# Residual loads two steps earlier and attention visits re-spaced in a strided-attention plus feed-forward kernel

## The chip, the cores and the metric

The kernel runs on one core of a Trainium2 chip. The metric is the device time of one execution in microseconds (us), lower is better. Times of several runs are given as a median with their lowest and highest; the profile is one further execution taken by the hardware profiler.

## What is computed

Attention over 8 batches, 8 heads, 576 positions, 64 wide: the first four heads see a causal band of 32 positions, the last four see causal positions at a stride of 32. Its output, as 4608 rows of 512, goes through a layer norm, a feed-forward of 512 to 2048 to 512 with ReLU, and a residual.

```
scores = np.where(masks, scale * q @ k.T, -1e9)
attn   = softmax(scores)
x      = (attn @ v) as rows of 512
out    = x + relu(layernorm(x) * g_ln @ w_ch1) @ w_ch2
```

## The kernel before

The feed-forward goes over 9 chunks of 512 rows (a chunk is the first 512 rows of a batch, the ninth gathers the eight remainders). A chunk has 16 steps, f = 0 to 15. One step of chunk c is: `ffn1` (L800 to L821), 12 matmuls of 128x512 into the one buffer `ph`; `h_high` on ACT (`hh`, L825) and `h_low` on DVE (`hl`, L830), which empty `ph`; one piece of attention work taken from a generator (`next(gen, None)`); then `second(*prev)`, that is `ffn2` (L840) of the step before, 12 matmuls into the four outputs `po`. At f = 15 of a chunk `ffn2` is followed by `finish` (L846, DVE), which adds the residual `x` and stores it; because of the lag by one step this lies in f = 0 of the next chunk. Every float32 product is made of three passes with high and low parts, hence the 12.

Chunk 0 follows an order written by hand (the string `ORDER`). Chunks 1 to 6 run the loop just described, and I number their steps 0 to 95 (step = 16 times (c - 1) + f). Chunks 7 and 8 run at the end in a different form, with seven products of half matrices (L1137) that need sums of weights and of x prepared during chunks 2 to 6.

The attention is spread over steps 0 to 95 by the generator `pieces` (L1017). Attention works on pairs of heads, four per batch, in the order strided, local, strided, local. Iteration i of the generator is a **visit**: its first piece (`m_piece`) issues on PE the score blocks of pair i + 1 (L444) and the value blocks of pair i (L513), on DVE the mask, the maximum and the division by the sums, on POOL the subtraction of the maximum (`s_sub`, L490), on ACT the exponential (L496), and on SP the store of pair i's result and the load of the v of pair i + 2. The second piece, one step later, loads pair i's result back transposed in blocks (`x_raw`, L592, from ACT's queue), sums and transposes the probabilities of pair i + 1 on DVE (L533 to L535, L609), stores them (`pd<-sm`, L613), transposes the q and k of pair i + 2 (L414, L419) and loads q and k of pair i + 3 (L355). The third piece loads the probabilities back (`pt<-pd`, L622 or L627) and makes the high and low parts of x for the feed-forward of the next chunk (`x_blocks`: L601 on DVE, L684 on ACT, L685 on DVE). A short visit has three pieces and loads a strided pair's `pt` already in the second one; a long visit has a fourth, empty piece. So the Boolean `short` (L1021) sets how many steps lie between visits.

Other work in the same steps:

- `RES_AT` (L1052) lists the four f at which the residual `x` of the chunk is loaded by SP (two DMAs each, L709 and L711); its variance follows three steps later (L716 to L721).
- In chunks 2 to 5, at f = 2 and f = 3, after `second`: `w_whole` (three stores on SP), `w_sums` on POOL (two additions L760, four L765) and `w_split` (four copies on ACT, L772; four subtractions on DVE, L773; four stores on SP, L775). I call the one at f = 2 the first split and the one at f = 3 the second.
- In chunk 6 the table `last_steps` (L1067) gives, by f, loads of the ninth chunk's rows (`tail`), their transposes (`turn`), half matrices (`half_x`) and differences (`sums_x`).

Each engine and each DMA queue runs its instructions in the order of the program; the last lines of the kernel pin that order.

Of the kernel before, what the change touches and what calls it, by code (L numbers as in the profile page):

```python
# [62 lines left out]
def kernel(  # L63
# [256 lines left out]
    NHP = H // 2  # L320
# [348 lines left out]
    def m_piece(p, nxt):  # L669

        ps = bank(f"m{(p or nxt).id}")
        parts = nxt.s_blocks(ps) if nxt else None
        av = p.v_blocks(ps) if p else None
        if nxt:
            nxt.s_masked(parts)
        if p:
            p.v_divide(av)
            p.v_store()
        if nxt:
            nxt.s_sub()  # L680
            nxt.s_exp()

    def split_x(hi, lo, src):
        nc.scalar.activation(out=hi, in_=src, func=AF.Copy)  # L684
        nc.vector.tensor_tensor(out=lo, in0=src, in1=hi.bitcast(F32), op=ALU.subtract)  # L685
# [15 lines left out]
    def x_load(c, i, name="x"):  # L701

        t = tkp.tile([P, DM], F32, tag="tk", name=f"{name}{c}_{i}")
        if c < B:
            parts = [(0, P, c, P * i)]
        else:
            parts = [(REST * j, REST, 2 * i + j, CH) for j in range(2)]
        for p0, n, b, r in parts:
            nc.sync.dma_start(t[p0:p0 + n, 0:DM // 2], xd_l[b][r:r + n, :])  # L709
            xs = xd_s[b][0:S].rearrange("(r t) d -> t r d", t=NB)  # L710
            nc.sync.dma_start(t[p0:p0 + n, DM // 2:DM], xs[r // STR:(r + n) // STR])  # L711
        return t

    def x_scale(x, name):
        st = stp.tile([P, 6], F32, tag="st", name=f"st{name}")
        nc.vector.bn_stats(st, x)  # L716
        mv = stp.tile([P, 2], F32, tag="mv", name=f"mv{name}")
        nc.vector.bn_aggr(mv, st)
        rs = stp.tile([P, 1], F32, tag="rs", name=f"rs{name}", bufs=2 * NT)
        nc.vector.tensor_scalar(rs, mv[:, 1:2], 1e-6, None, op0=ALU.add)  # L720
        nc.gpsimd.tensor_tensor(out=rs, in0=rs, in1=mhalf, op=ALU.pow)  # L721
        return rs

    def tail_raw(cc):

        t = tkp.tile([P, CH], F32, tag="tk", name=f"xt{cc}")
        tv = t.rearrange("p (b g e) -> p b g e", b=B, e=32)
        for j in range(4):
            c0 = P * (cc % (NHP // 2)) + 32 * j
            for g in range(REST // 32):  # L730
                if cc < NHP // 2:
                    r0 = CH + 32 * g
                    src = xd_l[:, r0:r0 + 32, c0:c0 + 32].rearrange("b t e -> t b e")
                else:
                    src = xd_s[:, 0:S, c0:c0 + 32].rearrange(
                        "b (t g) e -> t b g e", g=NB)[:, :, CH // 32 + g, :]
                nc.sync.dma_start(tv[32 * j:32 * j + 32, :, g, :], src)
        return t
# [15 lines left out]
    def w_sums(p):  # L754

        f = []
        for i in range(2):
            w = w1s[2 * p + i].bitcast(F32)
            f.append(tkp.tile([P, 2, 2 * P], F32, tag="tk", name=f"f{i}_{p}"))
            nc.gpsimd.tensor_tensor(  # L760
                out=f[i].rearrange("p d x -> p (d x)"), in0=w[:, 0], in1=w[:, 1], op=ALU.add)
        a11, a12, a21, a22 = f[0][:, 0], f[0][:, 1], f[1][:, 0], f[1][:, 1]
        for out, x, y, op in ((a22, a21, a22, ALU.add), (a21, a11, a21, ALU.subtract),
                              (a11, a22, a11, ALU.subtract), (a12, a12, a11, ALU.subtract)):
            nc.gpsimd.tensor_tensor(out=out, in0=x, in1=y, op=op)  # L765
        return dict(s1=a22, s3=a21, s2=a11, s4=a12)

    def w_split(p, sums):

        for name, src in sums.items():  # L770
            t = tkp.tile([P, 2, 2 * P], F32R, tag="tk", name=f"{name}_{p}")
            nc.scalar.activation(out=t[:, 0], in_=src, func=AF.Copy)  # L772
            nc.vector.tensor_tensor(  # L773
                out=t[:, 1], in0=src, in1=t[:, 0].bitcast(F32), op=ALU.subtract)
            nc.sync.dma_start(w_spot(p, name), t.bitcast(F32))  # L775
# [3 lines left out]
    def whole_tile(i, names):  # L779
        t = wp.tile([P, 2, CH], F32, tag=f"w1_{i}", name=f"whole{i}_{names[0]}")  # L780
        for n, name in enumerate(names):
            whole[name] = t[:, n]

    def half_x(f, name):

        pool = w_pools[int(f >= NF2)]
        t = pool.tile([P, 2, CH], F32R, tag=f"w1_{f}", name=f"half_{name}")
        halfs[name] = t[:, 0], t[:, 1]
        split_x(t[:, 0], t[:, 1], whole[name])
# [4 lines left out]
    def sums_x(j, eng):  # L794
        j = str(j)
        for out, x, y in (("t1", "b12", "b11"), ("t2", "b22", "t1"), ("t3", "b22", "b12"), ("t4", "b21", "t2")):
            sum_x(eng, out + j, x + j, y + j)
# [74 lines left out]
    NP = len(pairs)  # L872
# [144 lines left out]
    def pieces():  # L1017
        for i in range(2 * NHP - 1, NP):
            now = pairs[i] if i >= 2 * NHP else None
            nxt = pairs[i + 1] if i + 1 < NP else None  # L1020
            short = i < 3 * NHP - 1 or i >= NP - NHP  # L1021
            m_piece(now, nxt)
            if i + 2 < NP:
                pairs[i + 2].load_v()
            yield
            if now:
                now.x_raw(nc.scalar)
            if nxt:
                nxt.v_sums()
                nxt.p_turned()  # L1030
                if short and not nxt.local:
                    nxt.p_load(nc.sync)
            if i + 2 < NP:
                pairs[i + 2].t_piece()
            if i + 3 < NP:
                pairs[i + 3].load_qk()
            yield
            if nxt and not (short and not nxt.local):
                nxt.p_load(nc.scalar)
            if now and now.b == B - 1:  # L1040
                cc = now.h0 // 2
                if cc >= NHP // 2:
                    whole_tile(0, (f"b21{cc % 2}", f"b11{cc % 2}"))
                now.x_blocks(whole[f"b{1 + cc // 2}1{cc % 2}"])
            elif now:
                now.x_blocks()
            yield
            if not short:
                yield

    gen = pieces()
    RES_AT = 6, 7, 9, 10  # L1052
    ps_r_ctx.close()
    ps_m_ctx = ExitStack()
    ps_m = ps_m_ctx.enter_context(tc.tile_pool(name="ps_m", bufs=1, space=bass.MemoryType.PSUM))
# [3 lines left out]
    def tail(cc):  # L1059
        tails[cc] = tail_raw(cc)  # L1060

    def turn(cc):
        nc.vector.transpose(whole[f"b{cc // 2 + 1}2{cc % 2}"], tails.pop(cc))
# [1 line left out]
    tails = {}  # L1065
    wide = NCHUNK - 2
    last_steps = {  # L1067
        2: [lambda: tail(2)],
        3: [lambda: whole_tile(1, ("b220", "b120"))],
        4: [lambda: turn(2)],  # L1070
        5: [lambda: half_x(4, "b220"), lambda: tail(0)],
        7: [lambda: turn(0), lambda: whole_tile(2, ("t10", "t20")), lambda: whole_tile(3, ("t30", "t40")),
            lambda: sums_x(0, nc.gpsimd)],
        8: [lambda: half_x(5, "t10"), lambda: half_x(6, "t20"), lambda: tail(3)],
        9: [lambda: half_x(7, "t30"), lambda: half_x(8, "t40")],
        10: [lambda: whole_tile(1, ("b221", "b121")), lambda: turn(3), lambda: half_x(9, "b221")],
        11: [lambda: tail(1)],
        13: [lambda: turn(1), lambda: whole_tile(2, ("t11", "t21")), lambda: whole_tile(3, ("t31", "t41")),
             lambda: sums_x(1, nc.vector)],
# [4 lines left out]
    for c in range(1, wide):  # L1084
        xres = []
        for f in range(NFC):
# [8 lines left out]
            if 2 <= c < 2 + NFC // 4:  # L1095
                p = 2 * (c - 2) + int(f > 2)
                if f in (2, 3):
                    w_whole(p)
                    w_split(p, w_sums(p))
            if f in RES_AT:  # L1100
                xres.append([x_load(c, RES_AT.index(f))])
            if f - 3 in RES_AT:
                i = RES_AT.index(f - 3)
                xres[i].append(x_scale(xres[i][0], f"{c}_{i}"))
# [81 lines left out]
    for f in range(NFC):  # L1186
# [4 lines left out]
        if f in (5, 6, 8, 9):  # L1191
            i = (5, 6, 8, 9).index(f)
# [45 lines left out]
```

## Time and profile before

| | |
|---|---|
| median of 3 runs | 898.2 us (896.03 to 898.89) |
| the profiled execution | 899.77 us, its span 898.0 us |
| mean granted TensorE clock | 0.985 of full speed |
| PE busy, share of the span | 97% |
| DVE, ACT, POOL busy | 56%, 24%, 21% |

The span runs from the first to the last instruction on the core; the 1.8 us around it are not seen in the trace. Steps 0 to 95 (chunks 1 to 6) take from about 144 to 727 us of the span. In the rows further down, a time is the start in us from the beginning of the span, then the duration; "idle before" is the time that the engine stood still ahead of the row, with what ended it. A matmul row of PE lasts longer than its distance to the next one, since matmuls overlap.

### The profile page before, as it was taken

How to read it: one execution, taken by the hardware profiler on the slowest of the kernel's cores; microseconds unless marked ns; L12 is line 12 of the kernel's file. 1: busy time of each engine (PE TensorE's matmuls, PEld its weight loads, DVE VectorE, ACT ScalarE, POOL GpSimd, SP SyncE). 2: the span in 40 equal slices, each digit the busy share in tenths (PEclk: the TensorE clock that was granted, in tenths of full speed). 3: DMA queues.
4: the chain of work that ended last, by engine and by line, in shares of the span. 5: the costliest groups of instructions: out<-in, count | busy, mean ns of one | idle time of the engine just before them, and what ended most of it. 6: DMA issues, size and time to landing. Idle time of an engine off the chain costs nothing.

```text
span 898.0 us, 18544 instructions
## 1 busy us (share of the span) xinstructions
PE 873.1 (97%) x7405; PEld 717.0 (80%) x7405; DVE 499.8 (56%) x965; ACT 215.6 (24%) x367; POOL 193.0 (21%) x230
## 2 busy tenths in 40 slices
PE   6899999998999999999999999999999999999997
PEld 5688888887887888788888888888877888888886
DVE  5799985545465555535564547555555453333442
ACT  3786731111122111211121112211112121111121
POOL 4787850001141013301130015011003000000000
PEclk8799999999899999999999999999999999999999
DMA  9899764676659565955597567956474174442111
GB/s 181 183 293 273 248 118 100 124 143 143 119 136 267 119 123 119 264 122 122 95 270 160 121 112 196 237 119 125 115 137 116 38 257 131 142 147 74 51 44 47
DMA packets 367854, 133.12 MB, mean 148 GB/s; under 512 B 296469, under 2 KB 351897, under 8 KB 367769
## 3 DMA queue, kind: packets, MB, share of 16 engines
q1 hardware_dynamic: 284440, 117.06, 52.4%
q10 hardware_dynamic: 83328, 14.89, 9.3%
q8 instruction: 58, 0.95, 0.5%
q14 instruction: 28, 0.22, 0.1%
HBM read 89.10 MB, written 42.80 MB: 147 GB/s over the span
## 4 chain that ended last, share of the span: by engine, by line
PE 86%; DMA 6%; DVE 3%; SPq 2%; issue 1%; ACT 1%; ACTq 0%; DVEq 0%
PE po L840 40%; PE ph L813 20%; PE ph L820 10%; PE x L1137 8%; PE m L513 2%; PE m L444 2%; DMA v_s<-in_v_dram 1%; DMA pd<-sm 1%; DMA pt<-pd 1%; SPq L355 1%; DMA rows<-in_q_dram 1%; DMA out_dram<-x 1%; PE s L444 1%; DVE s L773 1%; DMA grow<-in_moe_g_ln_dram 1%
## 5 line engine op out<-in xcount | busy, mean ns | idle before, releaser
L840 PE MATMUL po<-w,hh 128*128 128x512 f32 x1152 | 360.8, 394 | 0.0
L840 PEld LDWEIGHTS po<-w,hh 128*128 128x128 f32 x1152 | 214.6, 189 | 45.5 <-issue 0.2
L840 PE MATMUL po<-w,hl 128*128 128x512 f32 x576 | 225.1, 391 | 0.0
L830 DVE SCALAR_TENSOR_TENSOR hl<-ph,hh 128x512 fp32r<-128x512 f32 x112 | 77.2, 689 | 192.0 <-ACT hh L825 191.8
L813 PE MATMUL ph<-xh,w 128*128 128x512 f32 x444 | 174.8, 394 | 2.0 <-DVE hl L830 2.0
L813 PE MATMUL ph<-xl,w 128*128 128x512 f32 x444 | 173.0, 390 | 0.0
L825 ACT ACTIVATE hh<-ph 128x512 fp32r<-128x512 f32 x112 | 66.7, 596 | 294.5 <-PE ph L820 240.4
L840 PEld LDWEIGHTS po<-w,hl 128*128 128x128 f32 x576 | 108.7, 189 | 23.2
L820 PE MATMUL ph<-xh,w 128*128 128x512 f32 x444 | 119.0, 390 | 0.0
L490 POOL TENSOR_TENSOR sm<-sm,mx 128x640 f32<-128x640 f32 (+1 forms) x31 | 39.4, 1271 | 332.1 <-DVE mx L485 328.8
L813 PEld LDWEIGHTS ph<-xh,w 128*128 128x128 f32 x444 | 83.4, 188 | 21.1 <-DVE hl L830 3.9
L820 PEld LDWEIGHTS ph<-xh,w 128*128 128x128 f32 x444 | 83.2, 188 | 17.5
L813 PEld LDWEIGHTS ph<-xl,w 128*128 128x128 f32 x444 | 83.4, 188 | 16.9
L721 POOL TENSOR_TENSOR rs<-rs,mhalf 128x1 f32<-128x1 f32 x36 | 19.8, 550 | 288.5 <-DVE rs L720 288.5
L496 ACT ACTIVATE sm<-sm 128x648 f32<-128x648 f32 (+1 forms) x32 | 23.8, 745 | 108.6 <-POOL sm L490 108.6
L1137 PE MATMUL x<-half_t,ring 128*128 128x512 f32 x192 | 47.2, 389 | 0.0
L1137 PEld LDWEIGHTS x<-half_t,ring 128*128 128x128 f32 x192 | 36.0, 188 | 7.5
L302 POOL TENSOR_TENSOR w<-r,w 128x512 fp32r<-128x512 f32 x29 | 38.0, 1321 | 8.3 <-ACT w L298 7.8
L685 DVE TENSOR_TENSOR xl<-xo,xh 128x512 fp32r<-128x512 f32 x20 | 13.9, 697 | 26.2 <-ACT xh L684 26.2
L485 DVE TENSOR_REDUCE mx<-sm 128x12 f32<-128x648 f32 (+1 forms) x32 | 26.3, 822 | 1.9
L563 DVE TENSOR_TENSOR xo<-m,den 64x64 f32<-64x64 f32 (+3 forms) x120 | 27.1, 290 | 0.1
L760 POOL TENSOR_TENSOR f<-w 128x512 f32<-128x512 f32 x16 | 21.0, 1323 | 28.0 <-DMA out_dram<-x 13.5
(146 smaller groups left out, 855.5 us busy)
## 6 DMA issues: line engine op xcount, KB each, us to landing
s<-in_moe_w_ch_dram SPq DMA_DIRECT2D x32, 512.0 KB
ring<-wd SPq DMA_DIRECT2D x28, 512.0 KB
out_dram<-x SPq DMA_DIRECT2D x32, 256.0 KB
wd<-s SPq DMA_DIRECT2D x32, 256.0 KB
raw<-in_q_dram SPq DMA_DIRECT2D x108, 72.0 KB
raw<-in_k_dram SPq DMA_DIRECT2D x108, 72.0 KB
wd<-w SPq DMA_DIRECT2D x24, 256.0 KB
xds<-xo SPq DMA_DIRECT2D x32, 162.0 KB
```

Source lines behind the costliest of these rows:

```text
L302: eng.tensor_tensor(out=t[:, 1], in0=self.w[i], in1=t[:, 0].bitcast(F32), op=ALU.subtract)
L444: nc.tensor.matmul(o, lhsT, rhs, start=True, stop=True, tile_position=(64 * h, pos))
L485: nc.vector.reduce_max(mx[:, :, 0:nt], sm, axis=AX.X)
L490: eng.tensor_tensor(out=sm, in0=sm, in1=mx[:, :, 0:nt].unsqueeze(3).broadcast_to([P, 2, nt, sm.shape[3]]), op=ALU.subtract)
L496: nc.scalar.activation(out=self.smv, in_=self.smv, func=AF.Exp, scale=SCALE)
L563: nc.vector.tensor_tensor(out=xo[r, t0:t1, h0:h1].rearrange("p t h d -> p h t d"), in0=av, in1=den[r, h0:h1, t0:t1].unsqueeze(3).broadcast_to(
L813: nc.tensor.matmul(ph, w1h[:, cc], x[:, cc, :], start=(new and n == 0 and i == 0), stop=False)
L820: nc.tensor.matmul(ph, w1l[:, cc], xt[c][0][:, cc, :], start=False, stop=(cc == NCC - 1))
L825: nc.scalar.activation(out=hh, in_=ph, func=AF.Relu)
L830: nc.vector.scalar_tensor_tensor(out=hl, in0=ph, scalar=0.0, in1=hh.bitcast(F32), op0=ALU.max, op1=ALU.subtract)
L840: nc.tensor.matmul(po[i], hx[:, cs], w, start=(f == 0 and n == 0), stop=(f == NFC - 1 and n == 2))
L1137: nc.tensor.matmul(ps, wx, xx, start=(start and j == 0 and i == 0), stop=(j == 1 and i == 2), skip_group_check=not start)
```

## The change

`RES_AT` goes from f = 6, 7, 9, 10 to f = 4, 5, 7, 8. The rule for short visits changes: before, all visits of the last batch are short (i = 28 to 31); now three single visits are (i = 15, 21, 29). The visits i = 7 to 11 stay at steps 0, 3, 6, 9, 12. From i = 12 on they come at

| i | before, step | now, step |
|---|---|---|
| 12 to 15 | 16, 20, 24, 28 | 16, 20, 24, 28 |
| 16 to 19 | 32, 36, 40, 44 | 31, 35, 39, 43 |
| 20 to 23 | 48, 52, 56, 60 | 47, 51, 54, 58 |
| 24 to 27 | 64, 68, 72, 76 | 62, 66, 70, 74 |
| 28 to 31 | 80, 83, 86, 89 | 78, 82, 85, 89 |

In the numbering of chunk 6 the last row is f = 0, 3, 6, 9 before and f = -2, 2, 5, 9 now. `last_steps` is moved to suit, most of its entries one step up.

```diff
-            short = i < 3 * NHP - 1 or i >= NP - NHP
+            short = i < 3 * NHP - 1 or i in (15, 21, 29)
...
-    RES_AT = 6, 7, 9, 10
+    RES_AT = 4, 5, 7, 8
...
     last_steps = {
-        2: [lambda: tail(2)],
-        3: [lambda: whole_tile(1, ("b220", "b120"))],
-        4: [lambda: turn(2)],
-        5: [lambda: half_x(4, "b220"), lambda: tail(0)],
...
+        1: [lambda: tail(2)],
+        3: [lambda: whole_tile(1, ("b220", "b120")), lambda: turn(2)],
+        4: [lambda: tail(0)],
+        5: [lambda: half_x(4, "b220")],
...
```

**The order on SP, chunk 1, steps 7 to 10.** The rows run from the store of pair 10's result (`xds<-xo`, step 9) to the store of pair 11's probabilities (`pd5`, step 10) and the loads after it. Before:

```order
L709 DMA x1_1_2657<-xdl_202 128x256
L711 DMA x1_1_2657<-xds_203 128x1x256
L581 DMA xds_203<-xo_196 54x6x128 x2
L400 DMA v_s_190<-in_v_dram 18x11x64 x2
L400 DMA v_s_190<-in_v_dram 18x10x64
L400 DMA v_s_190<-in_v_dram 18x11x64 x2
L400 DMA v_s_190<-in_v_dram 18x10x64
L709 DMA x1_2_2800<-xdl_202 128x256
L711 DMA x1_2_2800<-xds_203 128x1x256
L613 DMA pd5_206<-sm0_192 32x4x160 x4
```

And now:

```order
L709 DMA x1_2_2660<-xdl_202 128x256
L711 DMA x1_2_2660<-xds_203 128x1x256
L709 DMA x1_3_2702<-xdl_202 128x256
L711 DMA x1_3_2702<-xds_203 128x1x256
L581 DMA xds_203<-xo_196 54x6x128 x2
L400 DMA v_s_190<-in_v_dram 18x11x64 x2
L400 DMA v_s_190<-in_v_dram 18x10x64
L400 DMA v_s_190<-in_v_dram 18x11x64 x2
L400 DMA v_s_190<-in_v_dram 18x10x64
L613 DMA pd5_206<-sm0_192 32x4x160 x4
```

The load of an x between the v loads and the store of the probabilities is gone, and the fourth x now stands ahead of the store of the result.

**The order on POOL, chunk 3, f = 2 and 3.** The rows are the end of the first split's sums, and the second split's. Before:

```order
L765 TENSOR_TENSOR f0_2_4360<-f1_2_4362,f0_2_4360 128x256
L765 TENSOR_TENSOR f0_2_4360<-f0_2_4360 128x256
L760 TENSOR_TENSOR f0_3_4416<-w1_6_1286 128x512
L760 TENSOR_TENSOR f1_3_4418<-w1_7_1416 128x512
L765 TENSOR_TENSOR f1_3_4418<-f1_3_4418 128x256
```

And now:

```order
L765 TENSOR_TENSOR f0_2_4360<-f1_2_4362,f0_2_4360 128x256
L765 TENSOR_TENSOR f0_2_4360<-f0_2_4360 128x256
L490 TENSOR_TENSOR sm0_192<-sm0_192,mx4_3_4463 128x2x6x54
L760 TENSOR_TENSOR f0_3_4493<-w1_6_1286 128x512
L760 TENSOR_TENSOR f1_3_4495<-w1_7_1416 128x512
L765 TENSOR_TENSOR f1_3_4495<-f1_3_4495 128x256
```

The subtraction of visit 17, now at step 35, stands ahead of the second split's sums.

**The order on DVE, start of chunk 3 (f = 0, step 32).** The rows stand between `hl3_0` of f = 0 and the `finish` of chunk 2. Before, they are the visit's:

```order
L830 SCALAR_TENSOR_TENSOR hl3_0_4165<-ph3_0_4150,hh3_0_4163 128x512
L472 TENSOR_TENSOR sm1_193<-m4_2_4167,mask_l_112 128x2x4x64
L472 TENSOR_TENSOR sm1_193<-m4_2_4167,mask_l_112 64x128
L479 MEMSET sm1_193 32x2x32
L485 TENSOR_REDUCE mx4_0_4229<-sm1_193 128x2x5
L563 TENSOR_TENSOR xo_196<-m4_2_4167,den0_198 128x3x64
L563 TENSOR_TENSOR xo_196<-m4_2_4167,den0_198 128x2x64
L563 TENSOR_TENSOR xo_196<-m4_2_4167,den0_198 64x64
L563 TENSOR_TENSOR xo_196<-m4_2_4167,den0_198 128x5x64
L563 TENSOR_TENSOR xo_196<-m4_2_4167,den0_198 64x64
L846 SCALAR_TENSOR_TENSOR x2_0_3632<-po2_0_3303,rs2_0_3835,x2_0_3632 128x512
```

And now they are the second piece's:

```order
L830 SCALAR_TENSOR_TENSOR hl3_0_4244<-ph3_0_4229,hh3_0_4242 128x512
L533 TENSOR_REDUCE den1_199<-sm1_193 128x2x5
L534 TENSOR_SCALAR den1_199<-den1_199 128x2x5
L535 RECIPROCAL den1_199<-den1_199 128x2x5
L609 STREAM_TRANSPOSE sm0_192<-sm1_193 128x5x4x32
L419 STREAM_TRANSPOSE qt_s_178<-raw4_3_4068 128x18x32
L419 STREAM_TRANSPOSE kt_s_179<-raw4_3_4068 128x18x32
L846 SCALAR_TENSOR_TENSOR x2_0_3542<-po2_0_3303,rs2_0_3674,x2_0_3542 128x512
L846 SCALAR_TENSOR_TENSOR x2_1_3598<-po2_0_3303,rs2_1_3792,x2_1_3598 128x512
```

The visit has moved to step 31, and with it its second piece into the step of the `finish`.

## Rows read from the trace of the kernel before

**Rows 1.** The page's first part: busy time, share of span, instructions of PE.

```profile
PE 873.1 (97%) x7405; PEld 717.0 (80%) x7405; DVE 499.8 (56%) x965; ACT 215.6 (24%) x367; POOL 193.0 (21%) x230
```

**Rows 2.** The chain of waits, steps 43 to 45: start, duration (us), what.

```profile
412.30 2.72 PE po L840 x12
...
415.02 1.81 PE ph L813 x8
416.83 0.91 PE ph L820 x4
417.74 0.84 PE m L444 x44
418.57 0.90 PE m L513 x58
419.47 2.94 PE po L840 x12
...
425.14 2.72 PE po L840 x12
```

**Rows 3.** The timeline of PE at its idle places: start, duration, [idle before, releaser].

```profile
222.94 1.40 PE L513 MATMUL m<-v_l,pt 64*32 64x64 f32 x72 [2.46 <-DMA pt<-pd]
...
229.39 0.39 PE L813 MATMUL ph<-xh,w 128*128 128x512 f32 x1
...
367.10 0.50 PE L813 MATMUL ph<-xh,w 128*128 128x512 f32 x1 [1.23 <-DVE hl L830]
...
653.00 0.97 PE L513 MATMUL m<-v_l,pt 64*32 64x64 f32 x72 [1.29 <-DMA pt<-pd]
...
690.19 0.96 PE L513 MATMUL m<-v_l,pt 64*32 64x64 f32 x72 [1.32 <-issue]
```

**Rows 4.** Windows: us, busy of five engines, PEclk, DMA share, GB/s.

```profile
216.00:220.00 4.00, 4.00 (x45) 3.10 (x47) 0.91 (x3) 0.71 (x2) 0.00 (x0) 1.00 0.79 165
...
224.00:230.00 6.00, 6.00 (x31) 4.64 (x20) 3.70 (x12) 0.75 (x1) 1.83 (x2) 0.57 0.32 93
```

**Rows 5.** The timeline of SP, step 10: the store of pair 11's probabilities.

```profile
214.57 1.82 SPq L613 DMA_DIRECT2D pd<-sm  x4
```

**Rows 6.** The chain of waits ahead of PE's idle places at 222.94 and 653.00.

```profile
212.78 4.22 DMA x<-xds
...
218.90 4.00 DMA pt<-pd
...
649.63 3.33 DMA pt<-pd
```

**Rows 7.** The timeline of POOL: sums of a first split, and an undisturbed visit.

```profile
253.70 2.55 POOL L760 TENSOR_TENSOR f<-w 128x512 f32<-128x512 f32 x2
...
258.78 0.74 POOL L765 TENSOR_TENSOR f<-f 128x256 f32<-128x256 f32 x1
...
421.56 1.28 POOL L490 TENSOR_TENSOR sm<-sm,mx 128x648 f32<-128x648 f32 x1 [9.48 <-DVE mx L485]
```

**Rows 8.** The timeline of ACT at the end of a second split.

```profile
370.70 0.73 ACT L772 ACTIVATE s<-f 128x256 fp32r<-128x256 f32 x2 [0.24 <-DMA wd<-s]
371.34 0.58 ACT L825 ACTIVATE hh<-ph 128x512 fp32r<-128x512 f32 x1
```

**Rows 9.** The timeline of DVE: second piece, finish, end of a split, third piece.

```profile
210.10 0.81 DVE L533 TENSOR_REDUCE den<-sm 128x10 f32<-128x640 f32 x1
...
214.13 0.64 DVE L716 BATCH_NORM_STATS2 st<-x 128x6 f32<-128x512 f32 x1
...
349.59 2.71 DVE L846 SCALAR_TENSOR_TENSOR x<-po,rs,x 128x512 f32<-128x512 f32 x4
...
371.95 0.69 DVE L830 SCALAR_TENSOR_TENSOR hl<-ph,hh 128x512 fp32r<-128x512 f32 x1
...
409.74 0.69 DVE L685 TENSOR_TENSOR xl<-xo,xh 128x512 fp32r<-128x512 f32 x1 [0.70 <-ACT xh L684]
```

**Rows 10.** One line of the kernel, L773: duration in ns, min/median/max.

```profile
L773 DVE TENSOR_TENSOR s<-f,s x32: 411/424/1516, 267.3 to 563.0; 128x256 fp32r<-128x256 f32 x32
```

More of the change, by code (lines that the diff above doesn't have):

```diff
@@ L1067 @@
     last_steps = {
-        2: [lambda: tail(2)],
-        3: [lambda: whole_tile(1, ("b220", "b120"))],
-        4: [lambda: turn(2)],
-        5: [lambda: half_x(4, "b220"), lambda: tail(0)],
-        7: [lambda: turn(0), lambda: whole_tile(2, ("t10", "t20")), lambda: whole_tile(3, ("t30", "t40")),
+        1: [lambda: tail(2)],
+        3: [lambda: whole_tile(1, ("b220", "b120")), lambda: turn(2)],
+        4: [lambda: tail(0)],
+        5: [lambda: half_x(4, "b220")],
+        6: [lambda: turn(0), lambda: whole_tile(2, ("t10", "t20")), lambda: whole_tile(3, ("t30", "t40")),
             lambda: sums_x(0, nc.gpsimd)],
-        8: [lambda: half_x(5, "t10"), lambda: half_x(6, "t20"), lambda: tail(3)],
-        9: [lambda: half_x(7, "t30"), lambda: half_x(8, "t40")],
-        10: [lambda: whole_tile(1, ("b221", "b121")), lambda: turn(3), lambda: half_x(9, "b221")],
+        7: [lambda: half_x(5, "t10"), lambda: half_x(6, "t20"), lambda: tail(3)],
+        8: [lambda: half_x(7, "t30")],
+        9: [lambda: half_x(8, "t40"), lambda: whole_tile(1, ("b221", "b121")), lambda: turn(3)],
+        10: [lambda: half_x(9, "b221")],
         11: [lambda: tail(1)],
```

## The prediction

> **What bounds the kernel now.** I read the page first: PE is busy 97% of the span [rows 1], so time can only come from PE's last few idle microseconds, and any new idle place costs in full. The chain of waits shows the rhythm of steps 0 to 95 [rows 2]: `ffn1` 1.81 + 0.91 = 2.72 us, `ffn2` 2.72 us, and in a visit's step 1.73 us of small matmuls and an `ffn2` of 2.94. PE sets the pace wherever `hl` is ready in time, because `ph` is one buffer: `ffn1` of the next step waits until `hl` has read it. Between the end of one `ffn1` and the start of the next lie 2.72 us without a visit and 1.73 + 2.94 = 4.67 with one. In that time ACT must make `hh` and DVE `hl`, which takes 1.3 us (371.34 to 372.64 [rows 8, 9]). So an ACT or DVE delay of more than 1.4 us shows in a step without a visit, and only one of more than 3.4 us in a step with one. That margin decides this change.
>
> The timeline of PE then gives the idle places [rows 3]. At 222.94 (step 12) PE waited 2.46 us for `pt`, and afterwards ran at a granted clock of 0.57 [rows 4], so part of that stretch was at 1.2 GHz in place of 2.4: from 222.94 to 229.39 are 6.45 us where [rows 2] gives 0.90 + 2.94 = 3.84. That place costs 2.46 + 2.61 = 5.1. At 367.10 (end of step 35) PE waited 1.23 for `hl`, at 653.00 (step 83) 1.29 and at 690.19 (step 89) 1.32 for `pt`; the value blocks after these last two took 0.97 and 0.96, against 1.40 at step 12, so they show no slower clock.
>
> **Part by part. What it can win.**
>
> 1. *Step 12.* The probabilities of pair 11 go out at 214.57 [rows 5], behind an x that takes 4.22 us to land [rows 6], and come back 4.00 us after their issue at 218.90. That x is now loaded at step 8, ahead of the result's store. SP is not freed by all of it: the store and six v loads now queue behind one more x, so I let `pd` go out only 0.4 earlier. Without the x in front I take for `pt` the 3.33 us of the same load at 649.63 [rows 6]. So `pt` is 0.4 + 0.67 = 1.1 earlier, the stall is 1.4, and as with 1.23 to 1.32 [rows 3] the clock should hold. Gain 5.1 - 1.4 = 3.7; bounds 0 (the x at step 8 delays just as much) and 5.1. The DMAs moved 165 GB/s there [rows 4]. The Trainium skill ("DMA: Bandwidth & Descriptors", section "Issuing engines are not separate DMA queues") says that DMAs of all issuing engines share the same 16 DMA engines and interleave; by that an x of 256 KB taken away would free some 1.6 us (an estimate from the page's rule and the row's rate) in place of 0.67, and the sum would be 0.9 lower. The 0.67 is measured, and I stay with it.
>
> 2. *Step 35.* The wait came from a third piece and a first split in one step (f = 2). In chunk 3 the third piece now comes at f = 1. Gain 1.2. (Chunk 2's visits at f = 0 and 4 stay, and so does its like.)
>
> 3. *Steps 83 and 89.* Both waits follow from short visits, where a local pair's `pt` is loaded in the step before its use. Visits 28 and 30 are long now, one 5.4-us step more than the 1.3 missing. Gain 1.29 + 1.32 = 2.6.
>
> Together -7.5.
>
> **What it costs.**
>
> 4. *A visit in the step of a second split* (steps 35 and 51). Before, visits came at f = 0, 4, 8, 12 of chunks 2 to 5, never at f = 2 or 3. Now POOL must do the visit's subtraction before the sums, as its order shows. Counted from the end of the step's `ffn1` (417.74 [rows 2]), the subtraction starts at +3.82 and ends at +5.10 [rows 7]; the sums take 253.70 to 259.52, 5.82 [rows 7], so the last is there at +10.9. ACT's copies stand ahead of the next step's `hh`, and from the last copy to the end of `hl` are 1.6 (half of 0.73, then 371.34 to 372.64 [rows 8, 9]): +12.5. PE has until then 1.73 + 2.94 + 2.72 + 2.72 = 10.1, no visit in the following step helping. Idle 2.4, twice: +4.8. The bounds are 0, if POOL's spans (which the page calls rough) overstate the sums, and 3.5 with the next point's delay.
>
> 5. *A visit in the step of a first split* (step 66). The same 2.4, and now POOL goes on with the second split's sums beside the last L773, which takes 1516 ns at most against a median of 424 [rows 10]; the long ones are those beside a POOL addition. So 2.4 + 1.1 = 3.5, and 0.3 for the second split one step later, which starts from a late PE: +3.8.
>
> 6. *The finish behind a second piece* (steps 32 and 48). DVE's order puts the second piece between `hl` and `finish`. From the end of `ffn1`: 1.3 to the end of `hl`, 4.03 for the piece (210.10 to 214.13 [rows 9]), two of four L846 at 0.68 [rows 9]: 6.7. The next `ffn2` overwrites the first half of `po` and needs those two at 2.72 + 2.72 = 5.4. Idle 1.3, twice: +2.6 (bounds 0 and 1.7 each).
>
> 7. *The finish behind a third piece* (steps 64 and 80). In the trace's third piece at step 42 the last DVE row ends at 410.43 [rows 9]; two L846 after it end at 411.8, and PE's `ffn2` of the next step began at 412.30 [rows 2]. Nothing, with 0.5 to spare; if `pt` or the block load is late, what is late costs.
>
> 8. *Visit 21, short, behind the delay of 4.* Its second piece is 1.4 late against PE (2.72 less 1.3), and pair 22's `pt` has one step to arrive: 0 to 1.4, I take 0.4.
>
> 9. *The rest at nothing.* The other x loads and their variances run beside steps that have a spare step of slack; `last_steps` moves with the visits, its distances to them nearly kept. Their cover is SP's and DVE's idle time; gone, an x would delay a store by its two issues.
>
> Together +11.6, so +4.1 before the clock.
>
> 10. *The clock.* An idle 2.46 was followed by 2.6 us of slower matmuls, 1.32 and less by none [rows 3, 4]. The new 3.5 should cost it. The two of 2.4 are close to the 2.46; I count one of them: 2 x 2.6 = +5.2 (bounds 0 and 7.8).
>
> **Sum:** +9.3. The profiled execution took 899.77 (span 898.0 and 1.8 around it), 1.6 above the median of 898.2. So 909.1 for it, and **907.5** for the median.
>
> **The rivals.**
>
> - *Faster: the sums are done in time.* If the second split's last sum were ready at +8.5 in place of +10.9, points 4, 5, 8 and the clock vanish. Left are -7.5 + 2.6 = -4.9: **893.3**. For it: a late second split cost only some tenths in chunks 4 and 5 before. Against: there a visit in the next step gave PE 2 us of cover, which is now gone. Chance 0.10.
> - *The clock holds throughout:* +4.1, **902.3**. For it: three of four idle places left no mark. Against: the 2.46 did, and the 3.5 is longer. 0.20.
> - *The clock falls three times:* +11.9, **910.1**. For it: 2.4 is far nearer to 2.46 than to 1.32. 0.27.
> - *Step 12 does not change,* as the x of step 8 stands before the store and delays `pt` as the old one did: +13.0, **911.2**. For it: SP's queue is no shorter up to the store. Against: the 4.22-us load right in front of it is gone. 0.08.
>
> **How the numbers follow.** My forecast has 0.35. The range, 900.5 to 912.5, takes in all cases but the faster one, with an error of about 1.5 us. About 0.3%, 2.7 us, is what a measurement of this kernel can tell from no change. Faster is the first rival, 0.10; same needs the clock held and stalls at the low ends of their bounds, 0.07; slower has the rest, 0.83.
>
> **What would show it.** In the profile of the changed kernel PE should be idle about 1.4 before the value blocks at step 12, and not at all at steps 83 and 89's successors (82, 89). New idle places: about 2.4 ahead of `ffn1` at f = 5 of chunks 3 and 4, 3.5 ahead of f = 4 of chunk 5, each released by `hl`, with copies L772 just ahead of `hh` on ACT; and about 1.3 ahead of `po` at f = 1 of chunks 3 and 4, released by L846. After two of the longer ones the granted clock should fall below 1. I am wrong if those places show no wait for `hl`, or if the page's clock row stays at 9 between the second and the last slices and the time is below 900.

## The result

The changed kernel takes **906.42 us** (median of 4 runs, 905.44 to 908.5), the kernel before on the same chip 897.42 (4 runs, one more than in the table above, 896.03 to 898.89): ratio 1.0103 [1.0078, 1.0129], 9.0 us slower. On another chip, beside the experiments below, it was 907.26 against 894.44, ratio 1.015 [1.013, 1.0171]. The profiled execution took 906.15, its span 904.4; that of before had 898.0.

The page's first part, PE as in [rows 1]:

```profile
PE 873.1 (97%) x7405; PEld 716.3 (79%) x7405; DVE 499.2 (55%) x965; ACT 217.0 (24%) x367; POOL 192.7 (21%) x230
```

PE was busy for the same 873.1 us, in which matmuls at the lower clock count as busy. The 6.4 us more in the span are idle PE. The waits of PE between 186 and 800 us (waiting line, releaser: us in total, times, longest):

```profile
PE ph L813 <- DVE hl L830: 9.6, 5, 3.1
PE po L840 <- DVE x L846: 3.9, 3, 1.7
```

The waits for `pt` that [rows 3] show at three places (2.46, 1.29 and, put down to "issue", 1.32) are gone altogether; in their place PE waits for DVE. The timeline of PE gives the places (start, duration, [idle before, releaser]); the first row is the value blocks of step 12:

```profile
219.53 0.97 PE L513 MATMUL m<-v_l,pt 64*32 64x64 f32 x72
...
348.08 0.70 PE L840 MATMUL po<-w,hh 128*128 128x512 f32 x2 [1.71 <-DVE x L846]
...
371.87 0.50 PE L813 MATMUL ph<-xh,w 128*128 128x512 f32 x1 [2.51 <-DVE hl L830]
...
447.94 0.70 PE L840 MATMUL po<-w,hh 128*128 128x512 f32 x2 [1.71 <-DVE x L846]
...
471.73 0.50 PE L813 MATMUL ph<-xh,w 128*128 128x512 f32 x1 [2.51 <-DVE hl L830]
...
478.92 0.39 PE L813 MATMUL ph<-xh,w 128*128 128x512 f32 x1
...
548.24 0.70 PE L840 MATMUL po<-w,hh 128*128 128x512 f32 x2 [0.47 <-DVE x L846]
...
567.21 0.50 PE L813 MATMUL ph<-xh,w 128*128 128x512 f32 x1 [3.13 <-DVE hl L830]
...
574.42 0.39 PE L813 MATMUL ph<-xh,w 128*128 128x512 f32 x1
...
693.84 0.50 PE L813 MATMUL ph<-xh,w 128*128 128x512 f32 x1 [0.59 <-DVE hl L830]
```

Step 12 does not wait at all. The two 1.71 stand ahead of `po` at f = 1 of chunks 3 and 4, the two 2.51 ahead of `ffn1` at f = 5 of the same chunks, the 3.13 ahead of f = 4 of chunk 5: the five places that the prediction named. Together they are 11.6 us; the 0.47 and the 0.59 were not foreseen. (The fifth wait for `hl` in the list, 0.91 at 264.57 in chunk 2, was 0.78 in the kernel before.) The step from 471.73 to 478.92 lasts 7.19 us, that from 567.21 to 574.42 7.21, where a step without a visit has 5.44 by [rows 2]. The windows, read as [rows 4], say why:

```profile
372.00:376.00 4.00, 4.00 (x18) 3.31 (x19) 3.49 (x7) 0.60 (x1) 0.00 (x0) 1.00 1.13 323
...
472.00:476.00 4.00, 4.00 (x12) 3.14 (x12) 2.96 (x6) 0.00 (x0) 0.00 (x0) 0.61 1.10 318
...
568.00:572.00 4.00, 4.00 (x12) 3.13 (x11) 3.97 (x9) 1.81 (x5) 3.17 (x4) 0.57 0.91 227
```

After the second 2.51 and after the 3.13 the granted clock was at 0.61 and 0.57 (a part of the window at 1.2 GHz); after the first 2.51 it stayed at 2.4. Two falls cost 1.75 and 1.77.

What the 2.51 is made of stands in the chain of waits for steps 35 and 36 (start, duration, what):

```profile
358.34 0.91 PE ph L820 x4
...
363.00 1.28 POOL sm L490
364.28 2.51 POOL f L760 x2
...
369.37 0.80 POOL f L765
...
370.19 0.05 ACT s L772
...
370.58 0.52 ACT hh L825
...
371.12 0.70 DVE hl L830
...
371.87 2.11 PE ph L813 x8
```

The visit's subtraction on POOL runs ahead of the second split's sums, the last copy of the split on ACT starts when the last sum is there, and `hh` of the next step stands behind it.

### The profile page after: what moved, and what is told of

It is laid out like the page before. It is cut to its first block, busy times and chain, and to the rows that moved or that the text cites. A ratio compares the mean times of both kernels' runs of the same rounds, so it can differ in the third digit from the quotient of the medians.

```text
span 904.4 us, 18553 instructions
## 1 busy us (share of the span) xinstructions
PE 873.1 (97%) x7405; PEld 716.3 (79%) x7405; DVE 499.2 (55%) x965; ACT 217.0 (24%) x367; POOL 192.7 (21%) x230
## 4 chain that ended last, share of the span: by engine, by line
PE 83%; DVE 6%; DMA 5%; POOL 2%; issue 1%; SPq 1%; ACT 0%; ACTq 0%; POOLq 0%; DVEq 0%
PE po L840 38%; PE ph L813 20%; PE ph L820 10%; PE x L1138 8%; PE m L513 2%; PE m L444 2%; DMA xds<-xo 2%; DMA xraw<-xds 1%; DMA v_s<-in_v_dram 1%; DVE x L846 1%; POOL f L765 1%; DVE xo L563 1%; DVE mx L485 1%; DVE sm L472 1%; POOL f L760 1%
## 5 line engine op out<-in xcount | busy, mean ns | idle before, releaser
L685 DVE TENSOR_TENSOR xl<-xo,xh 128x512 fp32r<-128x512 f32 x20 | 13.9, 693 | 25.0 <-ACT xh L684 25.0
L773 DVE TENSOR_TENSOR s<-f,s 128x256 fp32r<-128x256 f32 x32 | 17.3, 566 | 18.4 <-ACT s L772 17.5
```

## The experiments

Ratios are to the kernel before, run beside each variant on the same chip. The kernel before had medians from 893.89 to 897.42 us in the four such sets, so the ratios are what is compared.

### The change in two halves

The x loads alone, on the kernel before:

```diff
-    RES_AT = 6, 7, 9, 10
+    RES_AT = 4, 5, 7, 8
```

> The kernel before with only RES_AT = 4, 5, 7, 8; visits and last_steps as before. My theory: the x loads alone end the stall at step 12, so PE has no idle place there and its 2.46 us and the 1.2-GHz stretch behind it are gone; steps 35, 83 and 89 stay. 892.3 to 895 us (897.4 less 2.5 to 5.1). Rival: step 12 was cured by something the visits did; then about 897.4 and the 2.46-us wait stays.

Measured: 894.45 against 895.93, ratio 0.9985 [0.997, 1.0]. That is 1.5 us, less than the 2.5 to 5.1 expected. No wait at step 12; the waits of steps 83 and 89 stay (0.99 and 1.97). The visits alone, on the changed kernel (`RES_AT = 6, 7, 9, 10` again):

> The changed kernel with RES_AT back at 6, 7, 9, 10, so only the visits and last_steps moved. My theory: all the new idle places stay (2.5 us twice ahead of f = 5 of chunks 3 and 4, 3.1 ahead of f = 4 of chunk 5, 1.7 twice ahead of po) and step 12 stalls again: 909 to 911.5 us. Rival: the slowdown comes from the x loads that now meet the visits' loads; then 897 to 900.

Measured: 908.61 on the same chip, ratio 1.0137 [1.0112, 1.0163], 0.4 below the range that was expected and far from the rival. The idle places are those of the changed kernel (1.71, 2.50, 1.72, 2.50, 3.13), and step 12 waits again:

```profile
221.74 0.97 PE L513 MATMUL m<-v_l,pt 64*32 64x64 f32 x72 [1.46 <-DMA pt<-pd]
```

So the visits carry the whole loss, and the earlier x wins at most some 0.3%. The 1.46 is not the 2.46 of [rows 3], though the order is the same there.

### The subtraction off POOL

```diff
-            nxt.s_sub()
+            nxt.s_sub(nc.vector if p and p.k in (17, 21, 25) else nc.gpsimd)
```

> The changed kernel with the subtraction of the maximum of visits 17, 21 and 25 on DVE in place of POOL, so that POOL's sums of weights no longer stand behind a visit. My theory: the idle places ahead of f = 5 of chunks 3 and 4 and f = 4 of chunk 5 go (8.1 us idle and some 3.5 of slower clock), the rest stays: 895 to 898 us. Rival: what delays hh there is the visit's own work on DVE and ACT (masks, division, exponential), to which 1.3 us on DVE is added; then 905 to 909.

Measured: 904.34, ratio 1.0089 [1.0069, 1.0109]. A miss. The 2.51s went, but one or two steps later a wait of 1.45 (ahead of `ffn1` of step 39) and, close together, two of 1.40 and 0.76 (step 54) came, and chunk 5 kept 2.20. The chain behind the 1.45:

```profile
368.79 4.38 DMA wd<-w
...
373.24 0.32 SPq L775
...
375.09 2.54 DMA pd<-sm
377.62 0.02 issue
377.64 2.78 DMA pt<-pd
...
381.79 0.61 DVE hl L830
```

The split's stores stand on SP ahead of the visit's probabilities (`pd`). An issue on SP waited for an earlier store to land (4.38 us), `pd` went out behind it, `pt` came late, and the third piece held up `hl`. POOL's order was the last of several things that the same step has to do; with that one taken away, PE waits for the next one.

### Visits at other places

```diff
-            short = i < 3 * NHP - 1 or i in (15, 21, 29)
+            short = i < 3 * NHP - 1 or i in (26, 27, 29)
```

The visits keep the places of the kernel before up to step 72 and then come at 75, 78, 82, 85, 89: the last four as in the change.

> The changed kernel with the short visits i = 26, 27, 29 in place of 15, 21, 29: visits at f = 0, 4, 8, 12 through chunk 4 and f = 0, 4, 8 and 11 in chunk 5, the last four as in the change. My theory: no visit meets a split or a finish as before, the gains at steps 12, 83 and 89 stay, and only some 0.5 us each at steps 80 and 88 are lost: 890.5 to 893.5 us. Rival: the new last_steps, the x loads or the long visits cost time by themselves; then 897 or more.

Measured: 892.29 against 895.93, ratio 0.9959 [0.9944, 0.9974]: faster than both kernels. The same with `RES_AT = 6, 7, 9, 10`:

> The variant with short visits 26, 27, 29, but with x loaded at f = 6, 7, 9, 10 as in the kernel before: the visits' part of that variant alone. Theory (the earlier x is worth what it was worth by itself, 1 to 2 us at step 12): 893 to 895. Rival (the earlier x is what makes that variant faster than the kernel before, by more than it does alone, because the visits of chunk 6 need it): 896 or more.

Measured: 891.3 against 893.89, ratio 0.9968 [0.9956, 0.998]. The time is below the range of the theory, on a chip where the kernel before is 2 us faster too; the rival is out. The two intervals overlap, so here the earlier x shows no gain. All that PE waits for in its profile (view of waits, 186 to 800 us):

```profile
PE ph L813 <- DVE hl L830: 2.0, 3, 0.9
PE m L513 <- DMA pt<-pd: 0.9, 1, 0.9
```

### Finish ahead of the second piece

```diff
+            early = f == 0 and c in (3, 4)
+            if early:
+                second(*prev)
             next(gen, None)
...
-            second(*prev)
+            if not early:
+                second(*prev)
```

> The changed kernel with one thing moved: at f = 0 of chunks 3 and 4 the second feed-forward product with its finish stands ahead of the second piece, not behind it. Theory (the two idle places of 1.71 ahead of po come from DVE's order, second piece before finish, the prediction's point 6): both go, and the second piece, some 2 us later on DVE, may hold up hl of the next step by 0.5 each; 903.5 to 905. Rival (DVE has too much in that step in any order, so the wait only changes its name from po to ph): 906 to 907.

Measured: 904.96 against 893.89, ratio 1.0116 [1.0096, 1.0137]; the changed kernel had 1.0103 and 1.015, so the time alone decides nothing. The trace does: the waits of 1.71 for L846 are gone, and one matmul group later, ahead of `ffn1` of f = 2, PE waits for `hl` instead:

```profile
347.88 0.50 PE L813 MATMUL ph<-xh,w 128*128 128x512 f32 x1 [0.76 <-DVE hl L830]
```

DVE's order made the 1.71; some 0.76 is DVE having too much in that step. The 2.51s and the 3.13 stayed, and the wait at step 64, which this edit does not touch, was 1.08 in place of 0.47.

### The splits moved away from the visits

```diff
-                p = 2 * (c - 2) + int(f > 2)
-                if f in (2, 3):
+                at = {2: 2, 3: 5, 4: 8, 5: 4}[c]
+                p = 2 * (c - 2) + int(f > at)
+                if f in (at, at + 1):
```

> The changed kernel with its visits where they are, but the two weight splits of chunks 3, 4 and 5 moved from f = 2, 3 to f = 5, 6, to 8, 9 and to 4, 5: into the third piece of a visit and the free step behind it, as they lay to the visits in the kernel before. Theory (points 4, 5 and 10: what costs is a visit in the step of a split, not the visits' new places as such): the idle 2.51, 2.51 and 3.13 go with the two falls of the clock (1.74 and 1.77), together 11.7, and up to three waits of 0.3 to 1.2 as at step 35 of the kernel before come in their place: 896 to 898.5. Rival (the visits' probability stores queue behind the splits' stores wherever these lie, as the run with the subtraction on DVE showed): 902 to 905.

Measured: 913.12, ratio 1.0216 [1.0196, 1.0236]. Some 15 us above the theory, and past the rival too. Chunk 5's 3.13 was gone as expected (f = 4, 5), but chunks 3 and 4 had worse; PE, then ACT and POOL, in the timelines:

```profile
391.90 0.79 PE L813 MATMUL ph<-xh,w 128*128 128x512 f32 x1 [4.74 <-DVE hl L830]
...
508.61 0.79 PE L813 MATMUL ph<-xh,w 128*128 128x512 f32 x1 [7.52 <-DVE hl L830]
...
506.07 0.42 ACT L772 ACTIVATE s<-f 128x256 fp32r<-128x256 f32 x1 [5.40 <-DMA wd<-s]
...
384.33 2.53 POOL L760 TENSOR_TENSOR f<-w 128x512 f32<-128x512 f32 x2 [14.73 <-issue]
```

Splits, x, `xraw` and `tail` share one pool of seven buffers (L99), and an x holds its buffer from its load until its output is stored in the next chunk's f = 0. A split takes six. Behind the x loads a copy of the split (506.07) waits until a store of its predecessor has landed. The row at 384.33 names no releaser. By the count of buffers (two x and six of the first split are more than seven) it too had to wait for one to come free, but the profile does not show which, so that half of the account is argued. With the finish edit besides, nothing changed:

> The two edits together on the changed kernel: splits moved to follow the visits, finish ahead of the second piece in chunks 3 and 4. Theory: the gains add, since the places are different steps: 893.5 to 896, that is level with the kernel before or a little faster, with only 0.5 to 1 us idle at any one place. Rival (the second piece behind the finish comes too late for what the moved splits need on DVE): no better than the moved splits alone.

Measured: 912.51, ratio 1.0214 [1.0196, 1.0231]: the rival.

So I put the splits ahead of the first x and off the visits: f = 1, 2 in chunks 3 and 4 (against the edit above).

```diff
-                at = {2: 2, 3: 5, 4: 8, 5: 4}[c]
+                at = {2: 2, 3: 1, 4: 1, 5: 4}[c]
```

> The changed kernel, visits in place, with the splits at f = 1, 2 in chunks 3 and 4 and at f = 4, 5 in chunk 5: again one in a third piece's step and one in the free step behind it, but in chunks 3 and 4 ahead of the first load of x, so that the seven buffers which splits, x and xraw share are not held by x's. Theory (points 4, 5 and 10): the idle 2.51, 2.51, 3.13 and the falls of the clock behind them go, 11.7 less up to three waits of about 1 us; 7 to 11 us below the changed kernel as measured in this same call. Rival A (the buffers: the x's of the chunk before hold four of the seven until their output is stored during f = 0, so the split's copies of f = 1 come late and hold up hh): a new wait of 2 us or more ahead of f = 2 of chunks 3 and 4, and only chunk 5's 3.13 with its clock gained, 3 to 5 us. Rival B (the visits' places cost by themselves): less than 2 us below it.

Measured: 898.95, ratio 1.0059 [1.0042, 1.0076], 8.3 below the changed kernel on the same chip (907.26). The 2.51s and the 3.13 are gone. Rival A's wait is there too, 2.00 and 1.20 ahead of f = 3; the chain behind the 2.00:

```profile
354.54 2.39 DMA out_dram<-x
...
357.02 0.43 ACT s L772
...
359.22 0.69 DVE hl L830
```

The copies wait for an x of chunk 2 to be stored. With the finish first, the x's buffers come free earlier:

> The run with the splits at f = 1, 2 and 4, 5, and besides the second product with its finish ahead of the second piece at f = 0 of chunks 3 and 4. In the earlier run of that edit alone the two idle places of 1.71 became two of 0.76. Theory: another 1 to 2 us below the moved splits alone, since the finish, and with it the x's that hold the buffers, comes 2 to 4 us earlier on DVE. Rival (the second piece and all that follows from it come later by as much): no better than the moved splits alone.

Measured: 893.44 against 894.44, ratio 0.9984 [0.9973, 0.9996]; 5.5 below the splits alone, where 1 to 2 were expected. The stores of the output start at 341.69 in place of 353.04, so the waits of 2.00 and 1.20 go along with the 1.71s. The waits of PE that are left from 186 to 800 us:

```profile
PE ph L813 <- DVE hl L830: 3.1, 5, 0.8
PE po L840 <- DVE x L846: 0.4, 1, 0.4
```

This kernel has the change's visits at the change's steps, and is 13.8 us faster than the changed kernel (907.26) on the same chip. The loss lies in what the visits meet, not in their spacing as such.

### The changed kernel again

> The changed kernel once more, nothing altered, on the chip of this call. Theory: the waits are set by the order of the instructions, so the ratio to the kernel before is again 1.010 (1.008 to 1.013), with the idle places of 1.71, 2.51 and 3.13 of equal length. Rival (a part of the 9 us is that of one chip or one call): 1.005 or less, or idle places of other lengths.

Measured: 907.26 against 894.44, ratio 1.015 [1.013, 1.0171], above the expectation, and its interval just misses that of the first measurement. Between the two the changed kernel's median differs by 0.8 us and that of the kernel before by 3.0, so the ratio moved mostly with the kernel before; why stays open. The lengths of the waits repeat to 0.01 (1.72, 2.50, 1.71, 2.50, 3.14), so they come from the order. The clock does not:

```profile
372.00:376.00 4.00, 4.00 (x12) 3.14 (x11) 2.45 (x5) 0.33 (x1) 0.00 (x0) 0.57 1.07 290
472.00:476.00 4.00, 3.34 (x15) 2.77 (x16) 3.89 (x7) 0.23 (x1) 0.00 (x0) 1.00 1.09 344
```

Here it fell after the first wait of 2.50 and not after the second, the reverse of the profile above.

## Why the prediction was right, point by point

Forecast 907.5, measured 906.42 and 907.26. By its own steps, from the two profiles:

| point | forecast | measured |
|---|---|---|
| 1, step 12 | -3.7 | -5.1 in this profile |
| 2, step 35 | -1.2 | -1.2 |
| 3, steps 83 and 89 | -2.6 | -2.6 |
| 4, visit and second split | +4.8 | +5.0 (2 x 2.51) |
| 5, visit and first split | +3.8 | +3.1 |
| 6, finish behind second piece | +2.6 | +3.4 (2 x 1.71) |
| 7, finish behind third piece | 0 | +0.5 |
| 8, visit 21 | +0.4 | 0 |
| 9, the rest | 0 | +0.6 |
| 10, clock | +5.2 | +3.5 (1.75 and 1.77) |

**Points 4 and 5** held step by step. From the end of `ffn1` (359.24) the subtraction starts at +3.76 and ends at +5.04, the last sum is there at +10.9 and `hl` at +12.6; forecast were +3.82, +5.10, +10.9 and +12.5. In chunk 5 the 3.13 is 0.4 short of the 3.5, for the most part because the last L773, beside a POOL addition, took 1.20 and not 1.5 us:

```profile
565.33 0.02 issue
565.35 1.20 DVE s L773
566.55 0.61 DVE hl L830
```

POOL's L760 next to it ran from 564.83 to 566.27, and the subtraction ended 0.28 after that. The Trainium skill ("SBUF — State Buffer", section "Who interferes with whom") says that a DVE instruction with two inputs in SBUF contends with a GpSimd instruction that reads SBUF. The row agrees: 1.20 against a median of 0.42 [rows 10].

What these points left out is that POOL was only the last wait of a crowded step. Taking POOL's part away gave 1 to 6 us by the ratios (1.0089 against 1.0103 and 1.015) and not the 8 to 11 that I then expected; taking the meeting itself away (splits at f = 1, 2 and 4, 5) gave 8.3.

**Point 6** was 0.4 low for each, at the upper bound of 1.7 that it gave. In DVE's timeline the second piece takes 4.3 us here, from 342.26 to the finish, and not the 4.03 of [rows 9]. The rows of DVE, with one of POOL:

```profile
342.00 1.56 POOL L765 TENSOR_TENSOR f<-f,f 128x256 f32<-128x256 f32 x2
343.11 0.48 DVE L534 TENSOR_SCALAR den<-den 128x10 f32<-128x10 f32 x1
...
345.52 1.25 DVE L419 STREAM_TRANSPOSE kt_s<-raw 128x576 f32<-128x576 f32 x1
346.60 2.64 DVE L846 SCALAR_TENSOR_TENSOR x<-po,rs,x 128x512 f32<-128x512 f32 x4
```

The 0.3 is L534: it took 0.17 in the piece at 210.10 from which the 4.03 was read, where POOL was idle, and 0.48 here, where it ended at 343.59 with POOL's additions (343.56). The same happened in chunk 4 (0.48, ended 443.45, POOL 443.43). In the run with the finish first, where POOL's additions were over by 342.43, the L534 of chunk 3 took 0.17 again (343.96). So POOL, which the prediction had priced for the splits alone, has a share in the 1.71 too.

**Point 7** named its own exception, "if `pt` or the block load is late, what is late costs". At step 64 the store of the probabilities took 3.22 us to land, L846 stood behind the third piece, and 0.47 was lost. **Point 9** was wrong in one place: "its distances to them nearly kept" does not hold at f = 9 of chunk 6, where two L685 of `half_x` and a variance now stand ahead of `hl` and cost 0.59.

**Point 1** undersized the gain of this pair of profiles, and oversized the typical one. SP's row that answers [rows 5]:

```profile
211.52 1.78 SPq L613 DMA_DIRECT2D pd<-sm  x4
```

Against PE (whose value blocks could have started at 220.48 before and start at 219.53 now) the probabilities go out 2.1 earlier; I took 0.4. Their stores landed within 1.9 us each, before within 2.9 to 3.6 (the last one 2.9), and `pt` took 3.75 against 4.00: together 1.25 where I took 0.67. So most of what was missed, 1.7 us, was the order on SP. The sentence on the Trainium skill's rule of shared DMA engines ("DMA: Bandwidth & Descriptors", section "Issuing engines are not separate DMA queues") had pointed to a larger gain than the 0.67, and the trace agrees with its direction (1.25). But the stall itself varies: with the old x it was 2.46 (and the clock fell), 1.46 and 0.94 in three profiled runs of three kernels; with the new x none in seven, and 0.33, 0.35 and 1.17 in three. The mean gain, without the clock, is then some 1.4, which is what the x loads alone gave (1.5 us, interval up to nothing). The profile of before had one of its long stalls: 899.77 is above every one of its 3 runs shown.

**Point 10** had the number of falls right (the 3.13 and one of the two others) and the price too high for this profile: 1.75, not 2.6. The 2.6 came from [rows 4], where the granted clock stayed low until about 229, twice as long as here. Neither price is fixed by the wait: in the run with the finish ahead of the second piece the same 3.13 was followed by a step of 8.42 us, 2.98 more than 5.44. The rival with three falls was seen too, in the run of the visits alone; the rival in which the clock holds, in none of the four profiles with these waits. The faster rival ("sums done in time") fell: they are done to within 0.1 where they were forecast.

One of the signs was badly chosen. The page's row of the clock reads 9 in all 40 slices, though it fell twice: a slice is 22.6 us, too coarse. The view of windows, some 4 us wide, shows it.

The sum against the profile of before was +9.3, and the span grew by 6.4: the gain at step 12 was 1.4 more and the clock 1.7 less than forecast. (The table's second column sums to +7.2; the rest lies ahead of step 12, whose value blocks could start 0.95 earlier in the profile of after.) The forecast for the profiled execution, 909.1, was 3.0 above the 906.15. That the median came out closer, 1.1, is in part luck: 1.6 was taken off for the long profile of before, while the profile of after lies within 0.3 of its median, and a typical stall at step 12 would have left less to gain.

## What to carry to other kernels

Moving work by a step in a schedule that is bound by one engine is priced by what it will share its new step with: here the visit's and the split's queues on POOL, ACT, DVE and SP all met, and clearing one of them only moved the wait. Before moving work out of a meeting, count the buffers it holds and who gives them back: with seven shared buffers the same splits cost 14 us more at one place than at another (ratios 1.0216 and 1.0059). A stall read from one profile is one draw: three profiles with the same order at step 12 had 2.46, 1.46 and 0.94.

## What the runs showed that I had not expected

- **Equal waits of PE were followed by TensorE's lower clock in one place and not in another.** Of eight waits of 2.50 or 2.51 in four profiles (the change twice, the visits alone, the finish edit), five were followed by 1.2 GHz and three not, in no fixed order; the four of 3.13 or 3.14 all were. Elsewhere a wait of 2.00 was followed by it (splits at f = 1, 2), and so was a pair of 1.40 and 0.76 at step 54 (the subtraction on DVE); one of 2.20 (the same run) and one of 2.61 (splits moved, with the finish edit) were not. So the length of the wait alone does not decide it; what does stays open.
- **The price of a fall varies with how long the clock stays low.** It was 1.75 and 1.77 in the change, 2.6 at step 12 of the kernel before, and 2.98 in the run with the finish ahead of the second piece, where the clock was low already when PE began again. The step there, in the timeline of PE:

```profile
564.73 0.79 PE L813 MATMUL ph<-xh,w 128*128 128x512 f32 x1 [3.13 <-DVE hl L830]
...
573.15 0.39 PE L813 MATMUL ph<-xh,w 128*128 128x512 f32 x1
```

- **An issue on SP waited for an older transfer.** In the run with the subtraction on DVE the store of a split went out only when a store issued 4.38 us before had landed, and the short store of the probabilities behind it paid.
- **A short DVE instruction lasted as long as the POOL addition beside it.** In the profiles of before and after L534 took 0.44 to 0.50 us in the seven places where it began during an L765 of POOL, and ended with it; in the other 41 it took 0.17.
